# Retention and gated MLP on one core: the product with w_out of four units in 2x2 blocks by Strassen's scheme, with loads and work in another order

## The chip, the cores and the metric

One core of a Trainium2 chip runs the whole program. The metric is device time in microseconds (us) of one execution. The kernel before takes 210.55 us (median of 3 runs, 210.35 to 210.76). One more execution was profiled; the rows below are from it.

## What is computed

Two stages. A retention layer (4 batches, 8 heads, 768 tokens, head size 64) carries a decayed state, and its output, heads side by side, is the input x (4 x 768 x 512) of a gated MLP.

```python
state = gamma * state + einsum('bhd,bhe->bhde', k[:, :, t], v[:, :, t])
y[:, :, t] = scale * einsum('bhd,bhde->bhe', q[:, :, t], state)
x = y.transpose(0, 2, 1, 3).reshape(B, S, H * D)
gate_pre = sum(conv_w[k] * xp[:, k:k + S, :] for k in range(5))   # xp: x behind 4 zero rows
gate = 1 / (1 + exp(-gate_pre))
val = x @ w_val
out = (gate * val) @ w_out
```

All numbers are float32.

## The kernel before, in words

The 768 tokens are cut into 6 chunks of 128; chunk n of all four batches is unit n (512 columns). A load brings q, k, v of one batch and chunk, numbered g = 0 to 23, four to a unit. A *visit* of g (functions `visit` and `rest_of_visit`, lines L377 to L450) is the attention of one load on TensorE (PE): 128 small 64x64 matmuls. POOL multiplies the v (for g = 0 to 3, the k) of every load by decay factors first (`decay`, L366), DVE turns the result into x (`evac`, L530).

For the two big products each float32 factor is split into a high part, rounded to fp32r on ACT, and the rest, a subtraction on POOL, and three of the four partial products are summed in PSUM: high by high, high by low, low by high. For x this is `round_x` (L540, ACT) and `rest_x` (L545, POOL: xl); for the gated value `round_gv` (L650, ACT: gvh) and `rest_gv` (L654, POOL: gvl).

Per unit there are four *val tiles* (letter V; `val`, L628), 12 matmuls of 128x128 by 512 columns, one for each 128 output channels, and four *out tiles* (letter O; `outp`, L662), 12 such matmuls, one for each batch. The gate of a tile is a convolution of five taps: the first on ACT (L611), four on DVE (`tap`, L613) into a PSUM tile `acc` (two buffers), then a sigmoid on ACT (L620). `gated` (L643, DVE) multiplies the val tile out of PSUM into the gate. `store` (L673, ACT) copies an out tile from PSUM to one of two buffers `o_sb`, and `send` queues its DMA. Val and out tiles share two PSUM banks, `mm`: a new tile waits until the one two before it has been read out. The last out tile is cut in two halves of 256 columns, so that its matmuls have that width.

The weights come as 64-bit floats in 8 pieces: 0 to 3 of w_val, 4 to 7 of w_out. Each becomes a float32 by bit operations: two passes on ACT (L567, L581), a shift on DVE (L573: top), a sum on POOL (L585: up), and then the split, ACT for the high part (L595), POOL for the low one (L599: wvl, wol).

The order is made ahead of time. The string WORK lists what PE does next (s, p, y, z: the first chunk; h: the head of the first visit; v: visit; V: val tile; O: out tile; w: a weight piece) and gives each step a due time; LOADS lists the first DMAs of SP's queue (q: q and k transposed, a: those and v, k: natural k, v: v, w: weight piece, t: small tables). `plan` then lays all steps out in one order for each engine by ranks from the due times, with fixed costs for each kind of step and with ring buffers as dependencies; steps may pass each other where nothing forbids it, so that the matmuls of two tiles can alternate. Every engine's queue then runs strictly in that order.

Of the kernel before, what the change touches and what calls it, by code (L numbers as in the profile page):

```python
# [16 lines left out]
P = 128  # L17
# [10 lines left out]
GV = 8  # L28
# [22 lines left out]
    ("q", 0), ("k", 2), ("k", 3), ("t", 0), ("v", 0), ("a", 1), ("k", 1),  # L51
    ("w", 1), ("a", 2), ("a", 3), ("k", 0), ("w", 0), ("w", 3), ("w", 2),
# [3 lines left out]
    "psysyzsyszzywzhVVwVVvwwOOvvOOvVvVVvVOOvvOVvv"  # L56
    "VVvOvVVVOvVvOOvvOVvvOOvOvOVVVVOVVOOVVOOOOO"
# [12 lines left out]
class Step:  # L70


    def __init__(self, due, engine, cost, reads, writes, fn, args):
        self.due, self.engine, self.fn, self.args = due, engine, fn, args
        self.cost, self.gap = cost if isinstance(cost, tuple) else (cost, cost)
        self.reads, self.writes = reads, writes
        self.waits, self.then = set(), []
        self.next = []
        self.after = []
        self.ready = 0.0  # L80
        self.own = 0.0
# [5 lines left out]
        self.other = None  # L87


def plan(steps, filler, last, into):  # L90
# [7 lines left out]
    for i, s in enumerate(steps):  # L98
# [126 lines left out]
    while any(free.values()):  # L225
# [32 lines left out]
        else:  # L258
            clock[e], end = start + s.gap, start + s.cost
# [14 lines left out]
def tile_retention_gated_mlp(  # L274
# [370 lines left out]
    def round_gv(n, m):
        gvs[n, m] = (
            mlp.tile([P, UT], F32R, name="gvh", bufs=GV),
            mlp.tile([P, UT], F32R, name="gvl", bufs=GV),
        )
        nc.scalar.copy(gvs[n, m][0], gate[n, m])  # L650

    def rest_gv(n, m, engine=nc.gpsimd):
        gvh, gvl = gvs[n, m]
# [158 lines left out]
    def conv(n, m, t):  # L812
# [16 lines left out]
    def val_tile(n, m, t):  # L829
# [13 lines left out]

    def out_tile(n, b, t, cols=1):
        width = DM // cols
        for q in range(cols):
# [7 lines left out]
            o = Slot("o" if cols == 1 else "gate", 2)  # L854
# [174 lines left out]
```

## Time and profile before

| | before |
|---|---|
| median of 3 runs | 210.55 us (210.35 to 210.76) |
| the profiled execution | 210.62 us, its span 208.8 us |
| PE busy | 199.4 us, 95% of the span |
| DVE, ACT, POOL busy | 119.0, 110.0, 106.3 us |

The span goes from the first to the last instruction; 1.82 us of the profiled execution lie around it. The matmul records overlap (each is some 400 ns long, and starts some 233 ns behind the one before it), so the pace of matmuls is read from the distance of their starts and not from their mean length. TensorE's granted clock is the upper one (2.4 GHz) in all 40 slices.

### The profile page before, as it was taken

What the parts mean: (1) busy time and instruction counts of PE and PEld (TensorE: products, weight loads), DVE (VectorE), ACT (ScalarE), POOL (GpSimd) and SP (SyncE); (2) the same over time, 40 slices, a digit from 0 to 9 for tenths busy, and PEclk for the clock granted to TensorE, in tenths of its full rate; (3) what the DMA queues carried; (4) which work ended last, traced back from release to release, by engine and by line L of the source; (5) the groups of instructions that cost most, each with busy time, mean ns of one, the idle gap of its engine ahead of it and who ended that gap; (6) DMA issues with size and microseconds to landing.
All of it is one profiled execution on the core that took longest, in us unless ns stands there. A gap on an engine that the chain in (4) does not pass through costs nothing.

```text
span 208.8 us, 7818 instructions
## 1 busy us (share of the span) xinstructions
PE 199.4 (95%) x3494; PEld 158.0 (76%) x3494; DVE 119.0 (57%) x180; ACT 110.0 (53%) x237; POOL 106.3 (51%) x93
## 2 busy tenths in 40 slices
PE   8796799999999999999999999999999999999994
PEld 3476568787887878787887887877777877888783
DVE  0465799922289912699749953269861189902000
ACT  2665967964377533776565653464732265431221
POOL 0479999999526490637665428064412233222200
PEclk9999999999999999999999999999999999999999
DMA  6999997668355316876462076671111100111122
GB/s 210 383 414 341 368 424 304 202 207 289 99 219 209 130 74 210 282 253 217 163 206 96 3 257 217 236 257 55 43 64 53 50 0 0 50 50 53 52 100 100
DMA packets 9253, 36.24 MB, mean 174 GB/s; under 512 B 1154, under 2 KB 1538, under 8 KB 6660
## 3 DMA queue, kind: packets, MB, share of 16 engines
q1 hardware_dynamic: 5472, 29.43, 38.8%
q10 hardware_dynamic: 3748, 6.32, 8.1%
q8 instruction: 27, 0.44, 0.9%
q14 instruction: 6, 0.05, 0.1%
HBM read 29.46 MB, written 6.29 MB: 171 GB/s over the span
## 4 chain that ended last, share of the span: by engine, by line
PE 79%; DMA 8%; DVE 7%; POOL 2%; issue 2%; ACT 1%; SPq 1%; ACTq 0%; POOLq 0%; DVEq 0%
PE mm L662 33%; PE mm L628 27%; PE sy L450 11%; DMA wst<-in_w_dram 5%; DVE acc L613 5%; PE sy L377 4%; PE z_ps L434 3%; DMA att<-in_att_dram 3%; POOL up L585 1%; DVE gate L643 1%; DVE top L573 1%; POOL wvl L599 1%; SPq L353 1%; DVE x L530 0%; ACT acc L567 0%
## 5 line engine op out<-in xcount | busy, mean ns | idle before, releaser
L613 DVE SCALAR_TENSOR_TENSOR acc<-x,cw_sb,acc 128x512 f32<-128x512 f32 x96 | 67.4, 751 | 4.9 <-ACT acc L611 4.3
L545 POOL TENSOR_TENSOR xl<-x,xh 128x512 fp32r<-128x512 f32 x24 | 30.9, 1287 | 37.5 <-ACT xh L540 37.5
L654 POOL TENSOR_TENSOR gvl<-gate,gvh 128x512 fp32r<-128x512 f32 x24 | 30.9, 1289 | 33.6 <-ACT gvh L650 33.5
L662 PE MATMUL mm<-woh,gvl 128*128 128x512 f32 (+1 forms) x100 | 38.1, 396 | 0.0
L662 PE MATMUL mm<-wol,gvh 128*128 128x512 f32 (+1 forms) x100 | 37.4, 389 | 0.0
L662 PE MATMUL mm<-woh,gvh 128*128 128x512 f32 (+1 forms) x100 | 37.3, 389 | 0.0
L628 PE MATMUL mm<-xl,wvh 128*128 128x512 f32 x96 | 34.1, 402 | 0.5 <-POOL xl L545 0.5
L366 POOL TENSOR_TENSOR att<-att,small_sb 128x512 f32<-128x512 f32 x24 | 25.3, 1058 | 17.2 <-DMA att<-in_att_dram 7.7
L628 PE MATMUL mm<-xh,wvh 128*128 128x512 f32 x96 | 33.4, 400 | 0.4 <-DVE gate L643 0.4
L673 ACT COPY o_sb<-mm 128x512 f32<-128x512 f32 x23 | 13.5, 586 | 28.6 <-PE mm L662 28.6
L643 DVE TENSOR_TENSOR gate<-mm,gate 128x512 f32<-128x512 f32 x24 | 16.5, 686 | 18.3 <-PE mm L628 16.1
L628 PE MATMUL mm<-xh,wvl 128*128 128x512 f32 x96 | 26.7, 396 | 0.0
L399 DVE TENSOR_TENSOR u<-sy,small_sb 128x512 f32<-128x512 f32 x20 | 13.7, 687 | 21.1 <-PE sy L377 13.2
L650 ACT CAST gvh<-gate 128x512 fp32r<-128x512 f32 x24 | 14.9, 620 | 15.7 <-DVE gate L643 15.5
L530 DVE TENSOR_TENSOR x<-sy,dec 128x512 f32<-128x512 f32 x20 | 13.7, 683 | 16.6 <-PE sy L377 10.9
L662 PEld LDWEIGHTS mm<-woh,gvl 128*128 128x128 f32 x100 | 18.7, 188 | 4.7 <-POOL gvl L654 0.3
L662 PEld LDWEIGHTS mm<-woh,gvh 128*128 128x128 f32 x100 | 18.7, 188 | 4.4 <-ACT o_sb L673 0.4
L628 PEld LDWEIGHTS mm<-xl,wvh 128*128 128x128 f32 x96 | 17.8, 187 | 5.2 <-POOL xl L545 0.9
L662 PEld LDWEIGHTS mm<-wol,gvh 128*128 128x128 f32 x100 | 18.7, 188 | 4.1 <-POOL wol L599 0.2
L628 PEld LDWEIGHTS mm<-xh,wvh 128*128 128x128 f32 x96 | 17.6, 188 | 5.2 <-DVE gate L643 0.8
L628 PEld LDWEIGHTS mm<-xh,wvl 128*128 128x128 f32 x96 | 17.9, 188 | 4.3
L620 ACT ACTIVATE gate<-acc 128x512 f32<-128x512 f32 x24 | 14.4, 600 | 12.5 <-DVE acc L613 6.1
(50 smaller groups left out, 238.5 us busy)
## 6 DMA issues: line engine op xcount, KB each, us to landing
att<-in_att_dram SPq DMA_DIRECT2D x20, 1024.0 KB, 5.4
out_dram<-o_sb ACTq DMA_DIRECT2D x23, 256.0 KB, 2.3
wst<-in_w_dram SPq DMA_DIRECT2D x8, 512.0 KB, 11.3
att<-in_att_dram SPq DMA_DIRECT2D x3, 768.0 KB, 8.4
att<-in_att_dram SPq DMA_DIRECT2D x5, 256.0 KB, 5.4
att<-in_att_dram SPq DMA_DIRECT2D x1, 512.0 KB, 3.7
out_dram<-gate ACTq DMA_DIRECT2D x2, 128.0 KB, 1.7
small_sb<-in_small_dram SPq DMA_DIRECT2D x1, 68.0 KB, 5.2
```

What stands on the lines that cost most here:

```text
L366: nc.gpsimd.tensor_tensor(v, v, vd_sb[:, c, :].unsqueeze(2).broadcast_to([P, 8, HALF]), op=ALU.mult)
L399: nc.vector.tensor_tensor(us[g], sy[:, :, 0:256].rearrange("p x (a t) -> p x a t", t=HALF), tri_sb.unsqueeze(1).unsqueeze(1).broadcast_to( ...
L450: nc.tensor.matmul(sy[cols, h, off:off + HALF], lhsT=lhsT, rhs=rhs, start=start, stop=True, skip_group_check=True,)
L530: nc.vector.tensor_tensor(xs[c][:, :, b, HALO:].rearrange("p (h j) t -> p h j t", h=2), y.rearrange("p h (j t) -> p h j t", t=P), decs[c]. ...
L545: nc.gpsimd.tensor_tensor(xl[n][:, :, b], xs[n][:, :, b, HALO:], xh[n][:, :, b].bitcast(F32), op=ALU.subtract)
L613: nc.vector.scalar_tensor_tensor(acc, x[:, :, k:k + P], cw_sb[:, m, k:k + 1], acc, op0=ALU.mult, op1=ALU.add,)
L620: nc.scalar.activation(gate[n, m], accs.pop((n, m)), AF.Sigmoid)
L628: nc.tensor.matmul(vps[n, m], lhsT=w[:, m, ct * P:(ct + 1) * P], rhs=xx[n][:, ct].rearrange("p b t -> p (b t)"), start=(i == 0), stop=(i = ...
L643: nc.vector.tensor_tensor(gv, vps.pop((n, m)), gv, op=ALU.mult)
L650: nc.scalar.copy(gvs[n, m][0], gate[n, m])
L654: engine.tensor_tensor(gvl, gate.pop((n, m)), gvh.bitcast(F32), op=ALU.subtract)
L662: nc.tensor.matmul(ops[n, b, cs.start][:, 0:cs.stop - cs.start], lhsT=gg[:, b * P:(b + 1) * P], rhs=w[:, ct, cs], start=(i == 0), stop=(i ...
```

## The change

Units 1 to 4 (SEVEN) no longer have out tiles. The gated value of such a unit is seen as 2x2 blocks (two halves of the channels by two pairs of batches), w_out as 2x2 blocks of 256x256, and the product is made by seven block products in place of eight (`product`: 12 matmuls of 128x128 by 256 columns each). Four block sums of the gated value (S1 to S4, `g_sum`) are made in place in the gate tiles on POOL; seven blocks are split (`g_round` on ACT, `g_low` on POOL) where four tiles were. Four block sums of w_out (`t_sum`) are made once on POOL, and their splits (`t_round` on ACT, `t_low` on POOL) lie in the buffers of the weight loads. For this the float32 w_out is held in one of the three x buffers until the sums are done. Results: one copy on ACT (p1), two sums on DVE (u2, u3), and four result blocks, one copied on ACT, three summed on DVE. Gate tiles now hold two tiles each, with three buffers (GU); gvl has seven buffers (GL).

LOADS and WORK are other lists. The sums could be put on DVE (SUM_DVE, LOW_DVE), but these lists are empty. The planner has new costs for the new steps. The diff, cut to its core:

```diff
-GV = 8
+GV, GL = 8, 7
+GU = 3
+SEVEN = (1, 2, 3, 4)
...
-    ("q", 0), ("k", 2), ("k", 3), ("t", 0), ("v", 0), ("a", 1), ("k", 1),
-    ("w", 1), ("a", 2), ("a", 3), ("k", 0), ("w", 0), ("w", 3), ("w", 2),
+    ("q", 0), ("t", 0), ("k", 0), ("v", 0), ("k", 2), ("a", 1), ("w", 0),
+    ("a", 2), ("k", 3), ("a", 3), ("w", 1), ("w", 2), ("k", 1), ("w", 3),
...
-    "psysyzsyszzywzhVVwVVvwwOOvvOOvVvVVvVOOvvOVvv"
-    "VVvOvVVVOvVvOOvvOVvvOOvOvOVVVVOVVOOVVOOOOO"
+    "spyzsyzsysyzwwzVVhwwvVVvOOOvOvvvVVvVVvTVOOVO"
...
+        elif n < NPAIR:
+            dst = up
+            full[n] = up.bitcast(F32)
+        else:
+            if n == NPAIR:
+                wo.append(xpool.tile([P, NPAIR, B, HALO + P], F32, name="x").rearrange(
+                    "p a b t -> p (a b t)"
+                )[:, 0:NPAIR * DM].rearrange("p (a n) -> p a n", n=DM))
+            full[n] = wo[0][:, n - NPAIR]
+            dst = full[n].bitcast(I32)
+        nc.gpsimd.tensor_tensor(dst, top, up, op=ALU.add)
...
+    TSUM = (
+        ((0, 0), (0, 1), (0, 0)),
+        ((0, 1), (1, 1), (0, 1)),
+        ((1, 1), (1, 1), (0, 0)),
+        ((1, 0), (1, 1), (1, 0)),
+    )
+
+    def t_sum(i):
+        dst, a, b = (quarter(*x) for x in TSUM[i])
+        nc.gpsimd.tensor_tensor(dst, a, b, op=ALU.subtract)
...
+    def t_round(k):
+        wt[k] = stage.tile([P, 512, 2], I32, name="wst", bufs=WB)
+        nc.scalar.copy(t_part(k, 0), quarter(*T_AT[k]))
+
+    def t_low(k):
+        nc.gpsimd.tensor_tensor(t_part(k, 1), quarter(*T_AT[k]), t_part(k, 0).bitcast(F32), op=ALU.subtract)
...
+    PLACE = {
+        A11: (0, 0), A12: (1, 0), A22: (1, 1), A21: (0, 1), S3: (0, 1), S2: (1, 1), S1: (0, 0), S4: (1, 0),
+    }
+    SUMS = {S3: (A11, A21, "subtract"), S2: (A22, S3, "subtract"), S1: (S2, A11, "add"), S4: (A12, S2, "subtract")}
+    PRODUCTS = (
+        (A11, 10, 0), (S2, 13, 1), (A12, 11, 0), (S3, 14, 1), (S1, 12, 0), (A22, 15, 1), (S4, 16, 0),
+    )
+    OPENS = (0, 1, 4, 5)
+    RESULTS = {2: (0, 0), 4: (1, 1), 5: (1, 0), 6: (0, 1)}
...
+    def g_sum(n, k, engine=nc.gpsimd):
+        a, b, op = SUMS[k]
+        engine.tensor_tensor(block(n, k), block(n, a), block(n, b), op=getattr(ALU, op))
...
+    def g_round(n, k):
+        nc.scalar.copy(g_part(n, k, 0), block(n, k))
+
+    def g_low(n, k, engine=nc.gpsimd):
+        low = g_part(n, k, 1)
+        engine.tensor_tensor(low, block(n, k), operands[n, k, 0].bitcast(F32), op=ALU.subtract)
...
+    def product(n, k, z):
+        a, w, bank = PRODUCTS[k]
+        if k in OPENS and z == 0:
+            banks[bank] = ps_m[0].tile([P, 512], F32, name="mm")
+        part, tc_ = divmod(z, 4)
+        tt, ct = divmod(tc_, 2)
+        g = operands[n, a, part // 2]
+        nc.tensor.matmul(
+            banks[bank][:, tt * 256:(tt + 1) * 256],
+            lhsT=g[:, ct, tt * P:(tt + 1) * P],
+            rhs=weight(w, part % 2)[:, ct],
+            start=(k in OPENS and z == 0), stop=(z == 11), skip_group_check=True,
...
+    def p1_copy(n):
+        held["p1"] = stage.tile([P, 512], I32, name="top").bitcast(F32)
+        nc.scalar.copy(held["p1"], banks[0])
+
+    def u2_sum(n):
+        held["u2"] = stage.tile([P, 512], I32, name="top").bitcast(F32)
+        nc.vector.tensor_tensor(held["u2"], banks[1], held["p1"], op=ALU.add)
+
+    def u3_sum(n):
+        nc.vector.tensor_tensor(held["p1"], banks[1], held["p1"], op=ALU.add)
+
+    def result(n, k):
+        o = outs[n, k] = mlp.tile([P, 512], F32, name="o_sb")
+        if k == 2:
+            nc.scalar.copy(o, banks[0])
+        elif k == 4:
+            nc.vector.tensor_tensor(o, banks[0], held["p1"], op=ALU.add)
+        elif k == 5:
+            nc.vector.tensor_tensor(o, held["p1"], banks[1], op=ALU.subtract)
+        else:
+            nc.vector.tensor_tensor(o, banks[0], held["u2"], op=ALU.add)
...
+        if m == 1:
+            split_block(d, A11, d + 0.1)
+            add(d + 0.15, S3)
+            split_block(d + 0.2, S3, d + 0.3)
+        elif m == 3:
+            split_block(d, A12, d + 0.15)
+            split_block(d + 0.05, A22, d + 0.1)
+            add(d + 0.2, S2)
+            split_block(d + 0.3, S2, d + 0.35)
+            add(d + 0.5, S1)
+            split_block(d + 0.55, S1, d + 0.6)
+            add(d + 0.7, S4)
+            split_block(d + 0.75, S4, d + 0.8)
```

### Where instructions moved

POOL, from the first piece of w_out to the last remainder of unit 0 (gvl; att: decay; up or x_554: a piece's sum; wol: its low part). Before:

```order
L599 TENSOR_TENSOR wol_92<-up_522,woh_91 128x512
L366 TENSOR_TENSOR att_430<-att_430,small_sb_86 128x512
L654 TENSOR_TENSOR gvl_629<-gate_544,gvh_628 128x512
L366 TENSOR_TENSOR att_443<-att_443,small_sb_86 128x512
L585 TENSOR_TENSOR up_535<-top_652,up_535 128x512
L654 TENSOR_TENSOR gvl_647<-gate_593,gvh_646 128x512
L599 TENSOR_TENSOR wol_92<-up_535,woh_91 128x512
L585 TENSOR_TENSOR up_641<-top_716,up_641 128x512
L585 TENSOR_TENSOR up_758<-top_719,up_758 128x512
L599 TENSOR_TENSOR wol_92<-up_641,woh_91 128x512
L599 TENSOR_TENSOR wol_92<-up_758,woh_91 128x512
L654 TENSOR_TENSOR gvl_722<-gate_669,gvh_721 128x512
```

And now:

```order
L608 TENSOR_TENSOR x_554<-top_509,up_524 128x512
L377 TENSOR_TENSOR att_438<-att_438,small_sb_86 128x512
L608 TENSOR_TENSOR x_554<-top_538,up_543 128x512
L620 TENSOR_TENSOR wol_92<-x_554,woh_91 128x512 x2
L705 TENSOR_TENSOR gvl_637<-gate_471,gvh_636 128x512
L608 TENSOR_TENSOR x_554<-top_667,up_631 128x512
L377 TENSOR_TENSOR att_442<-att_442,small_sb_86 128x512
L620 TENSOR_TENSOR wol_92<-x_554,woh_91 128x512
L608 TENSOR_TENSOR x_554<-top_754,up_661 128x512
L705 TENSOR_TENSOR gvl_750<-gate_644,gvh_749 128x512
L620 TENSOR_TENSOR wol_92<-x_554,woh_91 128x512
L705 TENSOR_TENSOR gvl_769<-gate_644,gvh_768 128x512
```

Before there are two decays in this piece, and both stand in its first four rows; now the two stand second and seventh, and the second low part of w_out, `wol_92<-x_554` in the x2 row, comes ahead of unit 0's second remainder.

PE, behind the end of the visits. Before (mm_2788: an out tile of unit 3, L628: val tiles of unit 4):

```order
L662 MATMUL mm_2788<-wol_92,gvh_2782 128x512
L662 MATMUL mm_2788<-woh_91,gvl_2783 128x512
L628 MATMUL mm_2811<-xh_2464,wvh_89 128x512 x2
L662 MATMUL mm_2788<-woh_91,gvh_2807 128x512
L662 MATMUL mm_2788<-wol_92,gvh_2807 128x512
L628 MATMUL mm_2811<-xh_2464,wvh_89 128x512 x2
L628 MATMUL mm_2811<-xh_2464,wvl_90 128x512 x2
L662 MATMUL mm_2788<-woh_91,gvl_2808 128x512
```

Now (L756: the last two products of unit 4, L679: the val tiles of unit 5):

```order
L756 MATMUL mm_3057<-wst_1195,gvh_2787 128x256 x8
L756 MATMUL mm_3057<-wst_1195,gvl_2824 128x256 x4
L756 MATMUL mm_3039<-woh_91,gvh_2971 128x256 x4
L756 MATMUL mm_3039<-wol_92,gvh_2971 128x256 x4
L756 MATMUL mm_3039<-woh_91,gvl_3020 128x256 x4
L679 MATMUL mm_3095<-xh_2658,wvh_89 128x512 x4
L679 MATMUL mm_3095<-xh_2658,wvl_90 128x512 x4
L679 MATMUL mm_3095<-xl_2681,wvh_89 128x512
L679 MATMUL mm_3112<-xh_2658,wvh_89 128x512
```

Before, out tiles stand between the val tiles of units 4 and 5; now all products of unit 4 stand ahead of unit 5's val tiles, and these follow each other.

DVE at the same place. Before (u: the last mask; x: the last two evacs; acc: taps of unit 5; gate: val tiles of units 3 to 4):

```order
L399 TENSOR_TENSOR u_2640<-sy_95,small_sb_86 128x2x256
L530 TENSOR_TENSOR x_2360<-sy_95,dec_1904 128x4x128 x2
L643 TENSOR_TENSOR gate_2533<-mm_2708,gate_2533 128x512
L643 TENSOR_TENSOR gate_2548<-mm_2724,gate_2548 128x512
L613 SCALAR_TENSOR_TENSOR acc_2756<-x_2360,cw_sb_87,acc_2756 128x512 x2
L643 TENSOR_TENSOR gate_2750<-mm_2741,gate_2750 128x512
L613 SCALAR_TENSOR_TENSOR acc_2756<-x_2360,cw_sb_87,acc_2756 128x512 x2
L613 SCALAR_TENSOR_TENSOR acc_2790<-x_2360,cw_sb_87,acc_2790 128x512
L643 TENSOR_TENSOR gate_2777<-mm_2760,gate_2777 128x512
L613 SCALAR_TENSOR_TENSOR acc_2790<-x_2360,cw_sb_87,acc_2790 128x512 x2
```

Now (top: u3 of unit 4; o_sb: its results; acc: taps of unit 5):

```order
L772 TENSOR_TENSOR top_2955<-mm_2944,top_2955 128x512
L663 SCALAR_TENSOR_TENSOR acc_3037<-x_2490,cw_sb_87,acc_3037 128x512
L663 SCALAR_TENSOR_TENSOR acc_3047<-x_2490,cw_sb_87,acc_3047 128x512
L779 TENSOR_TENSOR o_sb_3066<-mm_3039,top_2955 128x512
L663 SCALAR_TENSOR_TENSOR acc_3037<-x_2490,cw_sb_87,acc_3037 128x512
L781 TENSOR_TENSOR o_sb_3080<-top_2955,mm_3057 128x512
L663 SCALAR_TENSOR_TENSOR acc_3037<-x_2490,cw_sb_87,acc_3037 128x512
L783 TENSOR_TENSOR o_sb_3091<-mm_3039,top_2975 128x512
L663 SCALAR_TENSOR_TENSOR acc_3037<-x_2490,cw_sb_87,acc_3037 128x512
L663 SCALAR_TENSOR_TENSOR acc_3047<-x_2490,cw_sb_87,acc_3047 128x512 x2
L663 SCALAR_TENSOR_TENSOR acc_3105<-x_2490,cw_sb_87,acc_3105 128x512
```

Before, the taps of unit 5 alternate with the gating of unit 4's val tiles; now they alternate with the results of unit 4's products.

## Rows read from the trace of the kernel before

**Rows 1.** The page: engines, then 40 slices, then the chain by engine

```profile
PE 199.4 (95%) x3494; PEld 158.0 (76%) x3494; DVE 119.0 (57%) x180; ACT 110.0 (53%) x237; POOL 106.3 (51%) x93
...
POOL 0479999999526490637665428064412233222200
PEclk9999999999999999999999999999999999999999
...
PE 79%; DMA 8%; DVE 7%; POOL 2%; issue 2%; ACT 1%; SPq 1%; ACTq 0%; POOLq 0%; DVEq 0%
```

**Rows 2.** Busy time of PE, PEld, DVE, ACT, POOL in three stretches

```profile
10.00:23.00 13.00, 9.98 (x361) 8.36 (x361) 8.18 (x13) 8.62 (x18) 11.06 (x11) 1.00 0.95 365
23.00:48.90 25.90, 24.88 (x502) 19.32 (x503) 20.21 (x32) 18.98 (x41) 25.69 (x22) 1.00 0.77 290
48.90:100.00 51.10, 51.10 (x1099) 41.33 (x1101) 33.01 (x51) 30.27 (x69) 28.45 (x25) 1.00 0.55 198
```

**Rows 3.** The chain in order of time: start, length, what

```profile
1.64 5.40 DMA att<-in_att_dram
...
7.43 11.30 DMA wst<-in_w_dram
...
140.13 0.67 PE sy L450 x32
...
142.25 1.13 PE mm L628 x4
...
161.67 10.03 PE mm L628 x43
```

**Rows 4.** PE's matmuls of the output product alone, up to 48.9 us

```profile
23.00:48.90 25.90, 5.66 (x22) 3.95 (x23) 1.00 0.77 290
```

**Rows 5.** Timeline of PE: first and last matmuls of 256 columns

```profile
203.15 0.28 PE L662 MATMUL mm<-woh,gvh 128*128 128x256 f32 x1
...
205.52 0.28 PE L662 MATMUL mm<-woh,gvl 128*128 128x256 f32 x1
```

**Rows 6.** Timeline of the weight loads: the last one

```profile
205.40 0.19 PEld L662 LDWEIGHTS mm<-woh,gvl 128*128 128x128 f32 x1
```

**Rows 7.** Costliest groups: busy us, mean ns, idle before and its releaser

```profile
L613 DVE SCALAR_TENSOR_TENSOR acc<-x,cw_sb,acc 128x512 f32<-128x512 f32 x96 | 67.4, 751 | 4.9 <-ACT acc L611 4.3
L545 POOL TENSOR_TENSOR xl<-x,xh 128x512 fp32r<-128x512 f32 x24 | 30.9, 1287 | 37.5 <-ACT xh L540 37.5
L654 POOL TENSOR_TENSOR gvl<-gate,gvh 128x512 fp32r<-128x512 f32 x24 | 30.9, 1289 | 33.6 <-ACT gvh L650 33.5
...
L366 POOL TENSOR_TENSOR att<-att,small_sb 128x512 f32<-128x512 f32 x24 | 25.3, 1058 | 17.2 <-DMA att<-in_att_dram 7.7
...
L673 ACT COPY o_sb<-mm 128x512 f32<-128x512 f32 x23 | 13.5, 586 | 28.6 <-PE mm L662 28.6
L643 DVE TENSOR_TENSOR gate<-mm,gate 128x512 f32<-128x512 f32 x24 | 16.5, 686 | 18.3 <-PE mm L628 16.1
...
L650 ACT CAST gvh<-gate 128x512 fp32r<-128x512 f32 x24 | 14.9, 620 | 15.7 <-DVE gate L643 15.5
...
out_dram<-o_sb ACTq DMA_DIRECT2D x23, 256.0 KB, 2.3
```

**Rows 8.** Timeline of POOL in the conversion stage

```profile
25.44 1.30 POOL L585 TENSOR_TENSOR up<-top,up 128x512 int32<-128x512 int32 x1
26.69 1.05 POOL L366 TENSOR_TENSOR att<-att,small_sb 128x512 f32<-128x512 f32 x1
27.70 2.55 POOL L599 TENSOR_TENSOR wvl<-up,wvh 128x512 fp32r<-128x512 f32 x2
...
47.17 1.28 POOL L654 TENSOR_TENSOR gvl<-gate,gvh 128x512 fp32r<-128x512 f32 x1
```

**Rows 9.** Timeline of DVE near the end

```profile
157.85 0.69 DVE L530 TENSOR_TENSOR x<-sy,dec 128x512 f32<-128x512 f32 x1 [3.00 <-PE sy L450]
...
189.77 0.69 DVE L643 TENSOR_TENSOR gate<-mm,gate 128x512 f32<-128x512 f32 x1 [7.00 <-PE mm L628]
```

More of the change, by code (lines that the diff above doesn't have):

```diff
@@ L87, in __init__ @@
         self.other = None
+        self.keeps = []
+        self.two = False
 def plan(steps, filler, last, into):
@@ L103, in plan @@
                 rings.setdefault(k.ring, []).append((k, s))
-        for k in s.reads + s.writes:
+        for k in s.reads + s.keeps + s.writes:
             if isinstance(k, Slot):
@@ L258, in plan @@
         else:
+            if s.two:
+                start = s.start = max(start, clock["POOL"])
+                clock["POOL"] = max(clock["POOL"], start + s.gap)
             clock[e], end = start + s.gap, start + s.cost
@@ new lines, in val_tile, with names, keep, split_block @@
+        s = at(t + 3.0, "DVE", TIMES["DVE"], [bank], [gate_of, ("gt", n, m, 0), ("gt", n, m, 1)], gated, n, m)
+        s.keeps.append(mine)
+        d = t + 3.1
+        def names(*blocks):
+            return [("gt", n, 2 * PLACE[k][0] + i, PLACE[k][1]) for k in blocks for i in range(2)]
+        def keep(s, *blocks):
+            for h in sorted({PLACE[k][0] for k in blocks}):
+                s.keeps.append(gslots[n, h])
+        def split_block(due, k, low_due):
+            high, low = (Slot("up", 2), Slot("up", 2)) if k == S1 else (Slot("gvh", GV), Slot("gvl", GL))
+            ops_of[n, k] = high, low
+            keep(at(due, "ACT", TIMES["ACT"], names(k), [high], g_round, n, k), k)
+            reads = names(k) + [high]
+            if n in LOW_DVE and k in (S1, S2, S4):
+                s = at(low_due, "DVE", TIMES["DVE"], reads, [low], g_low, n, k, nc.vector)
+                s.two = True
+            else:
+                s = at(low_due, "POOL", TIMES["POOL"], reads, [low], g_low, n, k)
+            keep(s, k)
@@ new lines, in add @@
+        def add(due, k):
+            a, b, _ = SUMS[k]
+            if n in SUM_DVE:
+                s = at(due, "DVE", TIMES["DVE"], names(a, b), names(k), g_sum, n, k, nc.vector)
+                s.two = True
+            else:
+                s = at(due, "POOL", TIMES["POOL"], names(a, b), names(k), g_sum, n, k)
+            keep(s, a, b)
+        if m == 1:
[11 more added lines that the diff above has]
+            split_block(d + 0.75, S4, d + 0.8)
@@ L888, in tile_retention_gated_mlp @@
         convert(5.5, n)
+    products = [(n, k) for n in range(NU) for k in range(7 if n in SEVEN else NPAIR)]
     t, whole = 6.0, {}
-    now = dict.fromkeys("psyzvVO", 0)
+    now = dict.fromkeys("psyzvVOT", 0)
     now["h"] = now["v"] = B
```

158 lines of the change are left out of this document (133 added, 25 removed).

## The prediction

> **What bounds the kernel now.** I read the page first, then the stretches, the chain, and last the rows of the parts that change. The reader is to see in the page that PE is busy for 95% of the span at the full granted clock and stands for 79% of the chain, while POOL is full only in slices 3 to 10 and half empty later [rows 1]. The stretches say where that changes: from 48.9 to 100 us PE is busy for 51.10 of 51.10 us and POOL for 28.45; from 23 to 48.9 us POOL is busy for 25.69 of 25.90 us; from 10 to 23 us it still idles for 13.00 - 11.06 = 1.94 us [rows 2]. So POOL (behind the loads) bounds the kernel up to about 49 us, and PE from there to the end. What PE saves counts in the second part; what the new order of loads gives counts in the first only as far as POOL lets it.
>
> **PE's matmuls.** In the chain 43 val matmuls of 512 columns take 10.03 us, 0.2333 us each [rows 3]. Matmuls of 256 columns, each with its own weights, start 20 times between 203.15 and 205.52 us, 0.1185 us apart [rows 5]. A unit's out part was 4 x 12 x 0.2333 = 11.20 us and becomes 7 x 12 x 0.1185 = 9.95 us. Four units: **-5.0 us**. The trace shows the width itself, so I leave only 0.2 us either way for it.
>
> **The start.** The total loaded ahead of the visits is the same, 6.07 MiB. The third load landed at 7.04 us with 1.00 MiB issued up to it, the twelfth at 18.73 us with 5.07 MiB [rows 3]: 2.87 us per MiB. In the new list the first weight piece stands after 2.57 MiB, so its conversion is done early and PE's first val tile no longer waits for it; but the second piece ends at 4.82 MiB, some 18.0 us, and natural k of load 1 at 5.57 MiB, 20.2 us. POOL's queue is strict: it meets the sum of the second piece (behind one pass of ACT and one of DVE, some 0.6 and 0.69 us) at about 19.5 us and ends it at 20.8 us. From there to the last remainder of unit 0 its queue holds 23 instructions: 5 decays at 1.01 us and 18 others at 1.25 us, by the distances of their starts [rows 8], 27.55 us. That ends at 48.35 us. Before, the same remainder ends at 47.17 + 1.28 = 48.45 us [rows 8]. PE can have behind it by then all of two out tiles but the last matmuls (the two share the two banks, and each needs all four remainders), 24 matmuls, beside the four val tiles and three visits; before, it had 22 by 48.9 us [rows 4]. The lead is two matmuls: **-0.5 us**. If POOL's 1.94 us of idling all went, it would be -2.4 us; if the second piece landed 1 us later, +0.5 us. I take -0.5, since the sum of POOL's queue gives it. In SP's queue load 5 now stands behind three pieces of w_out: 6.07 + 1.00 + 1.50 + 1.00 = 9.57 MiB, 18.73 + 4.50 x 2.87 = 31.6 us, close to when visit 4 wants it (some 32 us, by the count of PE's matmuls); up to 1 us could be lost there, and it is in the range.
>
> **POOL's additions.** Each of the four units gets 4 block sums and 7 rests where 4 rests were, +28 instructions; the four sums of w_out and their four rests make +36 in all. A rest takes 1.29 us on POOL, a decay, which reads one full operand and one repeated, 1.06 us [rows 7]; block sums are not in the trace, and 1.06 to 1.29 us bound them: I take 1.29, as they read two full operands. POOL rises by 46.4 to some 153 us. Per unit PE needs 11.20 + 9.95 + 4 visits of 142.25 - 140.13 = 2.12 us [rows 3], 29.6 us; POOL needs 15 x 1.25 + 4 x 1.01 = 22.8 us. Slack: 6.8 us a unit. The tightest place is unit 4, since nothing of another unit is left to fill in. Behind its last val tile POOL has 9 instructions to the rest of S1 (two of them rests of x), 11.3 us, plus 0.9 us for the gating and 1 us for x: some 13 us. PE meanwhile has 8 + 24 + 36 + 12 matmuls of 256 columns, 9.5 us, and three visits, two of 2.12 us and the last without its scores, some 1.6 us: 15.3 us. I cost POOL's additions at **nothing**: PE's other work hides them, by 2.3 us there. If that cover goes, the excess is paid in full. The w_out sums hold an x buffer that the x of unit 3 takes next; their last rest stands some 23 us of POOL's queue behind 48.35 us, and unit 3's visits come after 80 us: nothing.
>
> **ACT and DVE.** ACT gets 16 more roundings of 0.62 us and 8 copies fewer of 0.59 us [rows 7], +5.2 us on 110. DVE gets 20 sums out of PSUM, which its gating shows at 0.686 us [rows 7], +13.7 us on 119. Neither is near the span. What counts is the wait that they add: products k and k+2 share a bank, and the second may not write until the sum or copy of the first is done. Cover is product k+1, 12 x 0.1185 = 1.42 us, where an out tile had 2.80 us. A DVE sum takes 0.69 us, and a tap in front of it 0.70 us (67.4 us for 96) [rows 7]: 1.39 us, about equal to the cover without signals. With a visit or a val tile between, as in most places, it is free. Bounds: 0, and 0.2 us for signals at all 20, 4.0 us. I take **+0.3 us**, near the lower end, since the order puts other matmuls at most of them.
>
> **The end.** Before, x of unit 5 was complete at 158.5 us, out tiles of unit 4 filled PE between the last val tiles, and DVE waited up to 7.00 us for PE [rows 9]. Now the last visit is followed by four products (5.7 us) and all val tiles of unit 5. The third val tile needs the bank of the first, so it waits for DVE's gating of that. From the end of the last visit: x after 0.8 us; DVE's queue then has u3, which waits for the fourth product and ends at 2.3 us; behind it 10 taps of 0.70 us and 3 results of 0.69 us, 9.1 us, ahead of that gating, which ends at 12.1 us. The third result writes the buffer of the first, whose DMA takes 2.3 us [rows 7]; this adds up to 0.5 us. PE is ready for the third val tile after 5.7 + 21 x 0.2333 = 10.6 us. **+1.4 us**, bounds 0 (taps in pairs overlap) and 2.0. Behind it the taps keep up: three to a val tile of 2.8 us.
>
> **The sum.** 210.62 - 5.0 - 0.5 + 0.3 + 1.4 = 206.8 us against the profiled execution, whose 210.62 us lie 0.07 us above the median and within the runs shown; so 206.8 us.
>
> **Rivals.**
> The start carries through. POOL's idle time up to 23 us goes [rows 2], and PE's earlier first val tile is kept: -2.4 in place of -0.5, 204.9 us. For it: the first piece lands 2.5 MiB earlier. Against it: the queue of POOL above.
> The banks eat the gain. All 20 hand-overs cost 0.2 us: 206.8 + 3.7 = 210.5 us, no change. For it: 1.39 us against 1.42 us. Against it: the interleaving.
> POOL falls behind, slower. Block sums and rests read two pieces of 256 in place of one row of 512. POOL becomes the bound when 11 p + 9.0 = 29.6, p = 1.87 us an instruction, and eats the 3.8 us over four units at p = 1.96. At p = 2.5 us, twice 1.25, it is 11 x 0.63 x 4 = 28 us, some 234 us. Against it: L545 reads x in four pieces of 128 and takes 1287 ns, L654 reads whole rows and takes 1289 [rows 7]. POOL's pace seems not to depend on pieces.
> The weight loads show. A load is listed with 0.19 us [rows 6]; if it could not lie beside the matmul before it, 36 loads more per unit would cost 36 x 0.19 x 4 = 27.4 us, 234 us. Against it: matmuls 0.1185 us apart have such a load each, so it is hidden [rows 5, 6].
> The Trainium skill (TensorE: Matmul & The Clock Gate, section The mechanism) does say that a weight load overlaps with running matmuls only where the row groups differ, which these full 128-row loads do not, and (section LDWEIGHTS (loading the stationary operand)) gives 128 / 1.2 = 107 ns for one; by that the estimate would be 15.4 us more, some 222 us. The trace disagrees with that rule.
>
> **How the numbers follow.** Forecast 0.58 (205.2 to 208.3 us), start carried through 0.13, banks 0.16 (of it 0.06 within 0.2% of the kernel before), POOL behind 0.10, weight loads 0.01, something else slower 0.02. A difference of 0.2%, 0.4 us, is about what can be told from none here. Faster: 0.58 + 0.13 + 0.10 = 0.81; same 0.06; slower 0.13. The range takes in the forecast, most of the second case and most of the third: 204.7 to 210.2 us.
>
> **What would show it.** Right: product matmuls 0.12 us apart; POOL near 153 us busy in all and full until 48 us, with unit 0's last remainder at 48 us and PE at its second out tile; PE without gaps over 0.3 us from 50 us to the last visit; one gap of 1 to 1.5 us ahead of the third val tile of unit 5, ended by DVE's gating. Wrong: POOL rests ending waits of PE in units 1 to 4; block sums above 1.5 us; gaps at each product; a first half that ends 2 us earlier than counted, or a visit waiting for load 5.

## The result, and the profile after

| | before | after |
|---|---|---|
| median, first session | 210.66 us (210.35 to 211.00, 6 runs) | 208.07 us (206.22 to 209.28, 6 runs) |
| ratio, 95% interval | | 0.9888 (0.985 to 0.9926) |
| the profiled execution | 210.62 us, span 208.8 us | 206.22 us, span 204.0 us |
| second session, the same kernels | 210.43 us (15 runs) | 206.99 us (6 runs), ratio 0.9856 (0.9813 to 0.9898) |

The changed kernel is faster, as forecast, by 1.1%; its median lies 1.3 us above the 206.8 us predicted, while its profiled execution lies 0.6 us below. The ratio of the second session leaves out one run of the changed kernel, of 210.58 us, as a slow one. The runs of the first session lie 3 us apart, and the mean granted clock of TensorE orders them: 0.998 in the runs of 206.22 and 206.52 us, 0.991 at 207.94 and 208.21, 0.983 at 208.97 and 209.28. In the profiled execution, one of the two at 0.998, the clock is at its lower level only from 203.3 us on, behind the last matmul (200.9 us), where that costs nothing.

The page of the profiled execution, the lines that answer to [rows 1]:

```profile
PE 193.9 (95%) x3632; PEld 162.6 (80%) x3632; DVE 131.7 (65%) x200; ACT 113.4 (56%) x245; POOL 150.1 (74%) x129
...
POOL 0479999999999999999717999545993798105500
PEclk9999999999999999999999999999999999999999
```

The three stretches of [rows 2]:

```profile
10.00:23.00 13.00, 9.70 (x299) 7.37 (x291) 8.56 (x14) 10.23 (x21) 11.71 (x11) 1.00 1.02 411
23.00:48.90 25.90, 25.22 (x532) 19.48 (x532) 19.23 (x30) 18.16 (x41) 25.90 (x23) 1.00 0.72 279
48.90:100.00 51.10, 51.10 (x1189) 43.89 (x1179) 38.27 (x58) 33.91 (x78) 50.12 (x43) 1.00 0.56 202
```

PE is busy throughout from 48.9 to 100 us, as before. But POOL is now busy for 50.12 of these 51.10 us, where it was for 28.45 [rows 2]: PE's work still hides it, but it has hardly a pause left.

Products on PE's timeline:

```profile
150.34 1.10 PE L756 MATMUL mm<-wst,gvh 128*128 128x256 f32 x8
151.28 0.63 PE L756 MATMUL mm<-wst,gvl 128*128 128x256 f32 x4
151.75 0.86 PE L679 MATMUL mm<-xh,wvl 128*128 128x512 f32 x3
```

Twelve matmuls start within 151.75 - 150.34 = 1.41 us, 0.1175 us each. The groups of POOL's splits (the low parts of the blocks) and block sums; then the sum of the second weight piece, behind which the prediction counted 23 instructions, and the last of these:

```profile
L741 POOL TENSOR_TENSOR gvl<-gate,gvh 128x512 fp32r<-128x512 f32 x24 | 30.6, 1291 | 8.4 <-ACT gvh L737 8.4
L724 POOL TENSOR_TENSOR gate<-gate 128x512 f32<-128x512 f32 x16 | 20.5, 1288 | 0.5 <-DVE gate L694 0.4
```

```profile
18.81 1.27 POOL L608 TENSOR_TENSOR up<-top,up 128x512 int32<-128x512 int32 x1
...
46.22 1.29 POOL L705 TENSOR_TENSOR gvl<-gate,gvh 128x512 fp32r<-128x512 f32 x1
```

The end, on DVE and then on PE:

```profile
177.63 0.69 DVE L783 TENSOR_TENSOR o_sb<-mm,top 128x512 f32<-128x512 f32 x1 [0.35 <-DMA out_dram<-o_sb]
178.24 4.21 DVE L663 SCALAR_TENSOR_TENSOR acc<-x,cw_sb,acc 128x512 f32<-128x512 f32 x6
182.36 0.68 DVE L694 TENSOR_TENSOR gate<-mm,gate 128x512 f32<-128x512 f32 x1
```

```profile
181.61 0.40 PE L679 MATMUL mm<-xl,wvh 128*128 128x512 f32 x1
183.09 0.50 PE L679 MATMUL mm<-xh,wvh 128*128 128x512 f32 x1 [1.09 <-DVE gate L694]
```

From one start to the next PE loses 1.48 - 0.23 = 1.25 us ahead of the third val tile of unit 5, for DVE's gating. PE's waits in the whole execution:

```profile
PE mm L679 <- ACT xh L551: 1.5, 1, 1.5
...
PE mm L679 <- DVE gate L694: 1.1, 1, 1.1
...
PE mm L796 <- POOL wol L620: 0.2, 1, 0.2
```

No wait ends at a split or a block sum of units 1 to 4. The 1.5 us lie at 18.8 to 20.3 us, ahead of the very first val tile, and end with the rounding of x on ACT (L551); this wait matters below.

### The profile page after: what moved, and what is told of

It is laid out like the page before. It is cut to its first block, busy times and chain, and to the rows that moved or that the text cites. A ratio compares the mean times of both kernels' runs of the same rounds, so it can differ in the third digit from the quotient of the medians.

```text
span 204.0 us, 8159 instructions
## 1 busy us (share of the span) xinstructions
PE 193.9 (95%) x3632; PEld 162.6 (80%) x3632; DVE 131.7 (65%) x200; ACT 113.4 (56%) x245; POOL 150.1 (74%) x129
## 4 chain that ended last, share of the span: by engine, by line
PE 72%; DMA 14%; POOL 5%; DVE 3%; issue 3%; SPq 1%; ACT 0%; POOLq 0%; ACTq 0%; DVEq 0%
PE mm L679 26%; PE mm L756 18%; PE mm L796 10%; PE sy L461 10%; DMA att<-in_att_dram 9%; PE sy L388 4%; DMA wst<-in_w_dram 4%; PE z_ps L445 3%; DVE acc L663 2%; POOL wol L620 2%; POOL att L377 1%; DMA out_dram<-o_sb 1%; SPq L364 1%; POOL gvl L705 1%; POOL x L608 1%
## 5 line engine op out<-in xcount | busy, mean ns | idle before, releaser
L741 POOL TENSOR_TENSOR gvl<-gate,gvh 128x512 fp32r<-128x512 f32 x24 | 30.6, 1291 | 8.4 <-ACT gvh L737 8.4
L679 PE MATMUL mm<-xh,wvh 128*128 128x512 f32 x96 | 31.8, 404 | 2.5 <-ACT xh L551 1.5
L679 PE MATMUL mm<-xl,wvh 128*128 128x512 f32 x96 | 33.3, 398 | 0.0
L679 PE MATMUL mm<-xh,wvl 128*128 128x512 f32 x96 | 28.5, 397 | 0.0
L679 PEld LDWEIGHTS mm<-xh,wvh 128*128 128x128 f32 x96 | 17.3, 188 | 6.8 <-ACT xh L551 1.6
L724 POOL TENSOR_TENSOR gate<-gate 128x512 f32<-128x512 f32 x16 | 20.5, 1288 | 0.5 <-DVE gate L694 0.4
L679 PEld LDWEIGHTS mm<-xh,wvl 128*128 128x128 f32 x96 | 17.8, 188 | 3.9
L679 PEld LDWEIGHTS mm<-xl,wvh 128*128 128x128 f32 x96 | 17.9, 188 | 3.7
L551 ACT CAST xh<-x 128x512 fp32r<-128x512 f32 x24 | 14.8, 618 | 10.6 <-DVE x L541 10.2
L705 POOL TENSOR_TENSOR gvl<-gate,gvh 128x512 fp32r<-128x512 f32 x8 | 10.3, 1286 | 13.3 <-ACT gvh L701 13.3
L661 ACT ACTIVATE acc<-x,cw_sb 128x512 f32<-128x512 f32 x24 | 16.5, 693 | 1.2 <-DVE x L541 1.0
L511 ACT COPY turned<-sy 64x2 f32<-64x2 f32 x20 | 3.1, 155 | 24.2 <-PE sy L461 23.0
L456 ACT COPY snap<-z_ps 128x256 f32<-128x256 f32 x40 | 14.0, 374 | 3.8 <-DVE o_sb L783 1.8
L756 PE MATMUL mm<-wst,gvh 128*128 128x256 f32 x96 | 16.0, 283 | 0.0
```

Of the source, the lines that this page charges most:

```text
L551: nc.scalar.copy(xh[n][:, :, b], xs[n][:, :, b, HALO:])
L661: nc.scalar.mul(acc, x[:, :, 0:P], cw_sb[:, m, 0:1])
L679: nc.tensor.matmul(vps[n, m], lhsT=w[:, m, ct * P:(ct + 1) * P], rhs=xx[n][:, ct].rearrange("p b t -> p (b t)"), start=(i == 0), stop=(i = ...
L724: engine.tensor_tensor(block(n, k), block(n, a), block(n, b), op=getattr(ALU, op))
L741: engine.tensor_tensor(low, block(n, k), operands[n, k, 0].bitcast(F32), op=ALU.subtract)
L756: nc.tensor.matmul(banks[bank][:, tt * 256:(tt + 1) * 256], lhsT=g[:, ct, tt * P:(tt + 1) * P], rhs=weight(w, part % 2)[:, ct], start=(k i ...
```

## Experiments

### The kernel again, and the scheme taken out

`e0_again` is the changed kernel. `e8_plain` keeps the new loads and order:

```diff
-SEVEN = (1, 2, 3, 4)
+SEVEN = ()
```

(and WORK without T, the step of w_out's sums, and without three of the seven O, here the products, of each of units 1 to 4).

> The changed kernel once more, unchanged. Its six runs lay between 206.22 and 209.28 us and followed the mean granted clock of the span (0.998: 206.22 and 206.52; 0.991: 207.94 and 208.21; 0.983: 208.97 and 209.28), where the kernel before shows 1.000 and a spread of 0.65 us. Theory: the new order leaves TensorE idle somewhere long enough that the granted clock sometimes falls. Then runs of this kernel again lie in two or three groups, about 206.3, 208.1 and 209.1 us, each with its clock. Rival, chance in that session: all runs near 206.4 us at clock 0.998.

> Loads and work in the new order, but without Strassen's scheme: every unit has its four val tiles and four output tiles (the last four of the seven places of a unit's products), and no block sums. Theory, the gain is that of the matmuls: 4 x 1.25 = 5.0 us come back and the wait in the end (1.1 us) goes, about 210.2 us at clock 1.0. Rival, the new order of loads gives most of the gain: 208 us or less.

`e0_again`: 206.99 us (206.23 to 210.58). Three runs at clocks of 0.998 to 1.000 took 206.23 to 206.61 us; the other three, at 0.983 to 0.991, 207.36, 209.04 and 210.58 us. (The last has the clock of the run of 207.36 us, so its 210.58 us are not the clock's alone; what else it was stays open.) `e8_plain`: 210.51 us (209.56 to 213.34, 12 runs); its seven runs at 0.998 or more have a median of 209.71 us, the kernel before in the same session 210.21. So at the full clock the loads and the order are worth 0.5 us, and Strassen's scheme, with its wait in the end, 3.2 us: five runs of the changed kernel at 0.998 or more, in two other sessions, have a median of 206.5 us. (By the medians of the same runs' spans, 207.9 and 204.3 us, it is 3.6 us; see the sum below.) Five of the twelve runs of `e8_plain` lie at 0.984 to 0.992 too: the falls of the clock come with the new loads and order, not with the scheme.

### POOL: where is it tight?

```diff
-        engine.tensor_tensor(low, block(n, k), operands[n, k, 0].bitcast(F32), op=ALU.subtract)
+        for _ in range(2):
+            engine.tensor_tensor(low, block(n, k), operands[n, k, 0].bitcast(F32), op=ALU.subtract)
```

> Each of the 28 splits of the seven blocks (the low part, on POOL) is computed twice, one after the other: 7 x 1.25 = 8.8 us more of POOL's queue per unit, 22.8 + 8.8 = 31.6 us against the 29.6 us that PE needs. Theory (POOL's additions are hidden by 6.8 us a unit): the cover is gone by 2 us in each of units 1 to 4, and at the last products of unit 4 by some 3 us more (five more instructions between its last val tile and S1, 6.3 us, less the 2.75 us of slack there): +5 us against the changed kernel at the same clock, bounds +2 and +11. Rival, POOL's queue plays no part from 48 us on: 0. Rival, POOL is already the bound: 28 x 1.25 = +35 us.

`e3_low2` took 226.5 us (222.97 to 231.03); the fastest run, at a clock of 0.984, 16.5 us more than the 206.5 us above. The theory had +5, with +11 as its end: it fell. I then set the end of each split on POOL in the changed kernel's trace against the first matmul that reads it. The narrowest place is the low part of S2 in unit 1; here on POOL and on PE:

```profile
81.35 1.27 POOL L724 TENSOR_TENSOR gate<-gate 128x512 f32<-128x512 f32 x1
82.59 1.04 POOL L377 TENSOR_TENSOR att<-att,small_sb 128x512 f32<-128x512 f32 x1
83.59 1.30 POOL L741 TENSOR_TENSOR gvl<-gate,gvh 128x512 fp32r<-128x512 f32 x1
```

```profile
85.45 0.64 PE L756 MATMUL mm<-wst,gvl 128*128 128x256 f32 x4
```

It is ready at 84.89 us and read at 85.45: 0.56 us. In units 2 to 4 it is 1.52, 2.48 and 1.67 us; S1 of unit 4, which the prediction took for the tightest, has 2.78.

`e11_s2` doubles only three of the seven:

```diff
+        for _ in range(2 if k in (A22, A12, S2) else 1):
```

> Of each unit's seven low parts on POOL only three are computed twice: those of A22, A12 and S2 (3 x 1.25 = 3.75 us a unit). Theory by the trace of the changed kernel: the tightest place of POOL is the low part of S2, which the second product needs, 0.57, 1.52, 2.48 and 1.67 us ahead of its use in units 1 to 4; it comes 3.75 us later, so waits of 3.2, 2.2, 1.3 and 2.1 us, +8.8 us at the full clock and more with falls of the clock behind the waits. Rival, the reckoning of the prediction (6.8 us free per unit, the tightest place S1 of unit 4 by 2.3 us): +1.4 us. Rival, POOL as a whole is the bound: +15 us.

216.84 us in the run at a clock of 0.999, +10.3 us (theory 8.8, the prediction's reckoning 1.4); the median, with falls of the clock, is 219.38 us. Its waits of PE:

```profile
PE mm L757 <- ACT gvh L737: 4.0, 2, 2.1
PE mm L757 <- POOL gvl L742: 2.9, 3, 1.9
...
PE mm L757 <- ACT o_sb L778: 1.4, 1, 1.4
```

All six lie at the second product, of S2: 2.8, 2.2, 1.4 and 1.9 us in units 1 to 4, where the theory had 3.2, 2.2, 1.3 and 2.1. So S2 it is: its sum stands on POOL behind the splits of A22 and A12, and its rounding on ACT waits for that sum. In unit 3 it is the product's bank that comes last: the copy that frees it (o_sb) stands on ACT behind the roundings of S2 and S1, which wait for POOL. These 8.3 us are read from the profiled execution, at a clock of 0.976; what the rest of the 10.3 us is stays open.

### The end

```diff
-        o = outs[n, k] = mlp.tile([P, 512], F32, name="o_sb")
+        if (n, k) == (4, 6):
+            o = outs[n, k] = mlp.tile([P, 768], F32, name="u", bufs=2)[:, 0:512]
+        else:
+            o = outs[n, k] = mlp.tile([P, 512], F32, name="o_sb")
```

> The fourth result of unit 4 goes to a buffer of its own, so that it does not wait for the DMA of the result two before it. Theory: in the end the wait of DVE of 0.35 us for that DMA lies on the chain (queue of taps and results, then the gating that PE waits for): the gap of PE ahead of the third val tile of unit 5 falls from 1.1 to about 0.75 us, and the time by 0.35 us. Rival, the wait lies beside another: 0.

The gap fell from 1.25 to 0.82 us, and from PE's last matmul ahead of its wait within the last visit to its last matmul of all it takes 30.29 us where it took 30.73: -0.44 us, about as the theory had it. The time is 206.24 us (205.79 to 207.61; ratio to before 0.981, 0.9781 to 0.9838), and 205.79 to 206.25 in its four runs at clock 1.000.

`e7_tail` and `e9_end` reorder DVE's queue behind the last result:

```diff
+        order = plan(steps, filler, first_val[0], ("ye", "sc"))
...
+        new = [last[x] for x in (
+            ("tap", 5, 1, 2), ("tap", 5, 1, 3), ("tap", 5, 1, 4), ("gated", 5, 0),
+            ("tap", 5, 2, 1), ("tap", 5, 2, 2), ("gated", 5, 1), ("tap", 5, 2, 3), ("tap", 5, 2, 4),
...
+        queue["DVE"][-len(new):] = new
```

> Only VectorE's order in the end is changed: the gating of unit 5's first val tile stands two taps earlier, and the taps and gatings behind it follow in the order of the val tiles; all other engines keep their order. Theory (the 1.1 to 1.25 us gap of TensorE ahead of the third val tile is VectorE's queue and nothing else): the gap goes, and the end comes 1.2 us earlier: 205.1 us at clock 1.0. Rival, VectorE's work in the end is the bound whatever its order: the gap moves to the fourth val tile or the first output tile, 206.3 us.

The gap went and 0.80 and 0.56 us came back at the first output tile, for ACT's rounding and POOL's low part of the gated value. The time (211.85 us; 209.31 and 210.20 at clock 1.000) tells nothing of the end, since the start had changed too: the steps were emitted in another order, and PE's fillers no longer lie in its waits. By its profile PE has four idle pieces of 1.6 to 1.7 us there, where the changed kernel has one of 1.5, and ten of its twelve runs lie at 0.952 to 0.992.

`e9_end` leaves the start as it was, takes the buffer of `e1_osb3`, and turns two steps of ACT round as well:

```diff
+        s = act.pop(names.index(("round_gv", 5, 2)))
+        act.insert(names.index(("sigmoid", 5, 3)), s)
```

> Only the end is changed: the fourth result of unit 4 has a buffer of its own, VectorE's gatings of unit 5 stand ahead of taps that are needed later, and ScalarE rounds the gated third tile ahead of the sigmoid of the fourth; all engines keep their order up to the last visit, and emission keeps its order too. With VectorE's order alone (and a start that had changed with it) the gap ahead of the third val tile had gone, but 1.36 us of waits came back at the first output tile, where that rounding stood behind the sigmoid. Theory, queue order is all that was wrong: both waits go, the stretch from the end of the last visit to the end falls from 32.96 to 31.8 us, and the time to 205.1 us at clock 1.0. Rival, VectorE's work in the end (11 us of taps and gatings behind the last result) is the bound: waits of 1.2 us remain somewhere, 206 us.

205.92 us (205.65 to 208.64), 205.65 and 205.81 at clock 1.000. The same stretch takes 30.58 us, 0.15 less than in the changed kernel and 0.29 more than in `e1_osb3`. The gap ahead of the third val tile is gone. The last three gatings on DVE, with the taps between them, and PE's first wait:

```profile
183.19 0.69 DVE L694 TENSOR_TENSOR gate<-mm,gate 128x512 f32<-128x512 f32 x1 [0.63 <-PE mm L679]
183.80 2.19 DVE L663 SCALAR_TENSOR_TENSOR acc<-x,cw_sb,acc 128x512 f32<-128x512 f32 x3
186.06 0.69 DVE L694 TENSOR_TENSOR gate<-mm,gate 128x512 f32<-128x512 f32 x1
186.67 2.33 DVE L663 SCALAR_TENSOR_TENSOR acc<-x,cw_sb,acc 128x512 f32<-128x512 f32 x3
189.66 0.69 DVE L694 TENSOR_TENSOR gate<-mm,gate 128x512 f32<-128x512 f32 x1 [0.66 <-ACT gate L671]
```

```profile
190.40 0.50 PE L799 MATMUL mm<-woh,gvh 128*128 128x512 f32 x1 [0.56 <-DVE gate L694]
```

The theory fell: PE now waits for the last gating instead. But that is not yet the rival, DVE's work as the bound. Behind the last result DVE has 16 instructions left (12 taps, 4 gatings) whatever their order, and it idles among them: 0.63 us, since the second gating now stands ahead of taps and waits for PE, and 0.66 us for ACT's last sigmoid, which waits for the last tap. So this order moved the wait, and whether another one would remove it was not tried.

### The clock, and the place of code

> Four more filler groups of TensorE ahead of the first val tile, where it waits some 1.7 us (18.6 to 20.3 us) for the converted weights; nothing else is changed. Theory, the dips of the granted clock begin at that wait: no run falls below 0.995, all lie near 206.3 us. Rival, the dips begin elsewhere (the wait ahead of the third val tile of unit 5, or earlier in the start): the spread of 206.2 to 209.3 us remains.

```diff
         if i == 0:
             vps[n, m] = ps_m[0].tile([P, 512], F32, name="mm")
+        if n == m == i == 0:
+            for _ in range(4):
+                filler("sc")
```

None of ten runs fell below 0.999, but they took 207.52 to 210.22 us, so a spread of 2.7 us can come without any fall; its cause stays open. (The wait that the fillers close ends with x's rounding, as shown above, and not with the weights.) PE's timeline:

```profile
18.80 2.05 PE L831 MATMUL sy<-const-float32-0.0 128*128 128x128 f32 x16
...
74.06 0.40 PE L682 MATMUL mm<-xh,wvh 128*128 128x512 f32 x1
75.05 0.50 PE L682 MATMUL mm<-xl,wvh 128*128 128x512 f32 x1 [0.58 <-issue]
```

The fillers close the wait, and a stop of 0.99 - 0.23 = 0.76 us appears 54 us later that no semaphore ends.

```diff
     def warm_up(i):
+        for _ in range(16 if i == 0 else 0):
+            nc.tensor.matmul(ye[:, 0, 0:1], lhsT=warm.broadcast_to([P, P]), rhs=warm, start=True, stop=True)
```

> Sixteen more matmuls of one column stand at the very start of TensorE's program, where it waits for the first load anyway; the order of all engines is as in the changed kernel. The four filler groups ahead of the first val tile were as many instructions (16 matmuls and 16 weight loads), and with them TensorE stood still for 0.6 us at 74.5 us with no releaser and lost 0.4 us more by 141 us, 1.3 us in all at the full granted clock. Theory: that loss comes from the place that the instructions then have in the program's code (fetched in 16 KB pieces), not from the fillers' work: the same stall near 74.5 us and about +1.3 us here too (207.5 us in an execution at clock 1.0). Rival, the fillers themselves were late for something: no stall, 206.3 us at clock 1.0, and falls of the clock as in the changed kernel.

208.65 us (208.07 to 210.35), 208.07 to 209.26 at clock 1.000, with the stop again:

```profile
74.60 0.39 PE L679 MATMUL mm<-xh,wvh 128*128 128x512 f32 x1
75.39 0.50 PE L679 MATMUL mm<-xl,wvh 128*128 128x512 f32 x1 [0.40 <-issue]
```

It is 0.79 - 0.23 = 0.56 us long. In both kernels 1,626 matmuls and as many loads of PE's trace stand ahead of the stop. So it hangs on the place in the program, not on the fillers' work. Of the 2.1 us by which the last matmul is late against the changed kernel's profile, 0.6 us are there ahead of 73 us, 0.65 come with the stop, and 0.7 between 99 and 113 us; the causes of the first and the last stay open. The clock lay at 0.991 or 0.992 in three of twelve runs.

`e6_fat` and `e10_fill2` fill the same wait with two matmuls of 512 columns:

```diff
+        for _ in range(2 if n == m == i == 0 else 0):
+            nc.tensor.matmul(sy[:, 0], lhsT=zero.broadcast_to([P, P]), rhs=zero.broadcast_to([P, 512]), ...)
```

(`e6_fat` writes `vps[n, m]` instead; `e10_fill2` also has three long warm-up matmuls for ten, so that the number of instructions stays.)

> The 1.7 us ahead of the first val tile are filled with two matmuls of zeros of 512 columns (into the val tile's own bank, before its first matmul), 4 matmul records in place of the 16 of the earlier filler. Theory, the clock falls because TensorE idles there: all runs show 0.998 or more, and with only a quarter of the shift in the program the median is near 206.4 us. Rival, the falls come from elsewhere: runs at 0.991 and 0.983 remain, 208 to 209 us.

207.17 us (206.83 to 209.53), two of six runs at 0.992: inconclusive, since PE still idled 1.0 us ahead of the fillers, which waited for the bank, and the first val tile came 1.0 us later than in the changed kernel.

> Two matmuls of zeros of 512 columns stand ahead of the first val tile, into a bank that is free then, and three float32 warm-up matmuls of 432 columns take the place of ten of 512 columns in 16 bits, so that the number of TensorE's instructions up to there stays the same: no shift in the code. Theory (falls of the clock begin at the 1.7 us wait; the cost of the earlier fillers was the shift): no stall at 74.5 or 109 us, all runs at 0.998 or more, 206.2 to 206.6 us. Rival, falls begin elsewhere: runs at 0.991 with 208 us remain. Rival, the fillers themselves cost: 207.5 us at clock 1.0.

All four runs took 206.11 to 206.45 us, at 0.998 to 1.000; ratio to before 0.981 (0.9766 to 0.9855). PE's timeline shows no idle time left ahead of the val tile, and no stop later on:

```profile
17.74 0.61 PE L478 MATMUL ye<-u,att 64*64 64x128 f32 x22
18.28 1.99 PE L680 MATMUL sy<-const-float32-0.0 128*128 128x512 f32 x4
19.82 1.37 PE L684 MATMUL mm<-xh,wvh 128*128 128x512 f32 x4
```

> The changed order of the end and the two matmuls of zeros ahead of the first val tile together. Expected if the two are independent: 206.3 us less the 0.6 us that the end gave at clock 1.0, 205.7 us, and no run below 0.997, so that the median is that too (the changed kernel's was 208.07 and 206.99 us in two sessions). Rival, the fillers only put off the falls: runs at 0.991 and 207 to 208 us among them.

206.20 us (205.98 to 207.33), ratio 0.98 (0.9759 to 0.984); five of six runs at 0.999 or more, one at 0.992. So the median missed the expected 205.7 us by 0.5, and a run fell where none should have: the fillers make falls rare, and not impossible, and the order of the end adds next to nothing.

Counted over all runs of one kind, the clock lay under 0.995 in 5 of 66 runs of the kernel before, in 11 of 24 of the changed kernel and its two variants of the end with the same start (`e0_again`, `e1_osb3`, `e9_end`), and in 1 of 20 with the wait filled (`e2_fill`, `e10_fill2`, `e12_both`). `e5_shift` and `e8_plain`, which leave the wait as it is, have 3 and 5 of 12. A fall itself was caught in the profile of `e11_s2`, whose start is that of the changed kernel; busy time by stretch (PE first), and the granted clock third from the end:

```profile
18.40:20.00 1.60, 0.19 (x14) 0.05 (x4) 1.54 (x3) 1.60 (x5) 1.60 (x2) 0.98 1.03 412
20.00:23.30 3.30, 3.18 (x48) 2.34 (x52) 2.00 (x3) 3.30 (x7) 3.30 (x4) 0.50 0.99 398
23.30:84.70 61.40, 60.82 (x1434) 49.62 (x1426) 46.30 (x72) 42.56 (x97) 60.27 (x51) 1.00 0.64 228
84.70:86.80 2.10, 0.01 (x1) 0.01 (x1) 2.10 (x4) 0.68 (x2) 2.10 (x3) 1.00 0.75 300
...
88.20:95.00 6.80, 6.10 (x138) 5.46 (x137) 3.06 (x5) 3.30 (x8) 6.72 (x7) 0.50 0.10 33
```

PE idles from 18.4 to 20.0 us, and from 20.0 to 23.3 us it has the lower level, 1.2 GHz: 3.3 us at half speed, 1.65 us of work lost. The profile of `e3_low2`, with the same start, has the lower level from 20.25 to 23.66 us. Behind the wait at 84.7 us of `e11_s2` the clock falls again, for 6.8 us. The distance between the changed kernel's runs at 0.998 (206.4 us) and at 0.991 (208.1 us) is that of one such fall.

## Why the prediction was right, and where it was not

**What bounds it.** Right in kind: POOL up to 48 us (25.90 of 25.90 us busy from 23 us on), PE behind it.

**PE's matmuls, -5.0.** Right: 0.1175 us a matmul with a weight load each, so the rival of visible weight loads is out. With the end's +1.25 us, four units at -1.25 us make -3.75 us, and by the spans taking the scheme out cost 3.6.

**The start, -0.5.** Small: the second piece's sum began at 18.81 us, not 19.5, and the last remainder ended at 47.51 us, not 48.35. By 48.9 us PE had the 24 matmuls of output tiles that were counted, and 28 of a visit besides, some 0.4 us: -0.9 us. By run, `e8_plain` gives 0.5 us. Load 5 landed at 29.4 us, so it cost nothing. That the start carries through (-2.4) did not come.

**POOL's additions, nothing.** The cost was right, the working was not. Each instruction took the 1.29 us that I took. But the slack was reckoned by unit; the sums of w_out and their rests (8 instructions, 10.3 us, charged to no unit) stand in POOL's queue up to 70.4 us, and it has hardly a pause until 100 us; and the tightest place was put at S1 of unit 4. It is S2 in every unit, since the second product needs it and it stands behind the last val tile's gating: 0.56 us in unit 1. That this held was luck as far as the reckoning goes, since it did not look there. The rival of POOL falling behind was nearer than its 0.10 and its 1.87 us an instruction said.

**The hand-over of banks, +0.3.** 0: no gap at a product in the changed kernel's profile. No run shows the 0.2 us for signals of its upper bound.

**The end, +1.4.** 1.25 us, and as forecast the wait was for DVE's gating. The wait for a DMA was counted as up to 0.5 us; a buffer of its own took 0.43 off the gap. Another order of DVE moved the wait to the first output tile; whether the amount of DVE's work is the bound isn't shown.

**The sum.** By the profile -5.0 - 0.9 + 1.25 = -4.65 us; the spans differ by 4.8 us and the executions by 4.4 us, since 2.22 us lie around the span, where 1.82 us did. That belongs to the kernel and not to the run: it is 1.74 to 1.94 us in every run of the kernel before and of `e3_low2`, `e7_tail`, `e8_plain`, `e9_end`, `e11_s2` and `e12_both`, and 2.17 to 2.28 in every run of the others. Why, no run shows.

**What was missing.** A term of +1.6 us on the median (208.07 against 206.5): the falls of the clock. The profiled execution, without a costly fall, lies 0.6 us below the forecast, and the falls bring the median 1.3 us above it: that the median is no farther off is in part two misses that offset each other. I looked at the wait ahead of the first val tile only for what it delays, and put its further cost at nothing. In the kernel before, by the starts of its matmuls, PE has idle pieces of 1.27 and 1.15 us there with attention between them; now it has one of 1.67 us, and the clock falls in about half of the executions. That the wait sets off the falls rests on `e10_fill2`, `e2_fill` and the count above, and on the profile of `e11_s2`, where the fall begins in it. Why some executions fall and others don't, no run shows.

## What to carry over

Slack of a helper engine is to be read at each hand-over, from the end of its instruction to the first one that reads it, and not from its load per stage. A wait of PE that no longer delays anything can still cost: look what the granted clock does behind it, over several executions, and fill it with work that leaves the number of PE's instructions as it is. In a tail, another order of one queue can move a wait and not remove it: before that queue is called full, look for its own idle time, and for what ended it.

## What the runs showed of the hardware

Sixteen more matmuls with their loads made the profiled executions of `e2_fill` and `e5_shift` 1.3 and 2.1 us longer, and 0.76 and 0.56 us of that are a stop at the same instruction of PE's program. The page lists the program's fetches as a queue of their own (of the changed kernel):

```profile
q8 instruction: 28, 0.46, 0.9%
```

That is 28 pieces of some 16 KB. The kernel's planner reckons with a first piece of 94 matmuls, with their loads, and 127.5 in each one after it; 94 + 12 x 127.5 = 1,624 matmuls is close to the 1,626 ahead of the stop in both shifted kernels. The stop comes three matmuls behind a visit, which uses up instructions fastest (128 matmuls in 2.12 us, [rows 3]). That the stop is a wait for such a piece fits this and isn't shown, since no row names it. The Trainium skill (Runtime: NRT & Kernel Launch, section Instruction fetch mechanics) holds fetches to be mostly hidden; here 0.56 to 0.76 us of one would not be.
